# Weaving the top-32 searches of neighbouring score blocks, with the softmax in place in the score tile

## The chip, the core and the metric

The kernel runs on one core of one Trainium2 chip. The metric is the device time of one execution in microseconds. A core has five engines that each work through their own queue of instructions in order: TensorE (PE, matrix products; PEld is its weight load), VectorE (DVE), ScalarE (ACT), GpSimd (POOL) and SyncE (SP, which here only issues DMAs). A wait on a semaphore holds everything behind it on that engine.

## What is computed

Attention with a top-32 mask, then two feed-forward layers.

```
scores = scale * q @ k^T                       # 4 batches, 8 heads, 576 x 576, head size 64
kth    = 32nd largest score of each row
scores = where(scores >= kth, scores, -1e9); scores -= max
attn   = exp(scores) / (sum + 1e-9);  x = (attn @ v) as 2304 rows x 512
x = (sigmoid(x @ w_gate) * (x @ w_val)) @ w_out        # inner size 1536
x = relu(x @ w_in)^2 @ w_out2                          # inner size 2048
```

## The kernel before

The 2304 rows are 18 row tiles of 128. They are worked through in 12 chunks: chunks 0 to 5 hold one row tile each, chunks 6 to 11 two each. For each chunk, attention runs over four pairs of heads; one row tile with one head is a **unit**, 144 units in all, eight per row tile. While the two layers (the MoE, `moe32` for chunks 0 and 1, `moe` for the others) of one chunk run on PE, attention works on a later chunk. A scheduler sets the order of each engine's instructions from the program's priorities and dependencies; `attend` says how many units attention is ahead of the MoE.

A unit goes through these stations:

- `scores` (L357): PE multiplies queries and keys into PSUM, ACT copies the 128 x 576 scores into a tile `S` (L379). There are five such tiles (`SB`), and the keys (`kn`, L148) and values (`vm`, L191) that are prepared for later batches take theirs from the same five.
- `softmax` (L382): the **search** on DVE, seven steps: MAX8 (L392, eight largest of each row) four times and MATCH_REPLACE8 (L399, which strikes those eight out) three times between them. The first replacement reads `S` and writes a second tile `W` (three of them); the later steps read and write `W`. Each step waits for the one before it. A manual order (L394) keeps one unit's search whole: the first MAX8 of a unit comes after the last of the unit before.
- Still `softmax`: POOL makes a bias (L408), ACT writes Prelu of `S` into `W` (L411), which removes what lies below the 32nd, then Exp in `W` with the row sum (L413, or L427 in chunks 0 to 5).
- Chunks 0 to 5: `transpose` (L462) lets PE transpose `W` (L475, L477), and `values` multiplies with the values.
- Chunks 6 to 11 (`ci >= TCI`): `turn16` (L444) takes a reciprocal on DVE (L450), ACT writes the scaled probabilities as fp16 into the score tile `S` (L454), POOL scales `W` (L455) and writes the fp16 remainders into `S` too (L457), and a DMA on SP transposes them into `PT` (L459). `values16` (L500) then multiplies `PT` with the values on PE (L509), once per pair of heads and row tile, 48 times.

So before the change a late unit holds its `S` until the DMA transpose has read it, and its `W` until POOL's subtraction. In chunks 0 to 5 it holds `S` until the Prelu has read it and `W` until PE has transposed it. The generator `attention` (L1011) emits all this unit by unit. Its inner function `late` (L1126) places the late work by the search of the unit that is running: `turn` of the unit before behind the third MAX8, and `tail` (the value products) of the unit two before behind the last.

Of the kernel before, what the change touches and what calls it, by code (L numbers as in the profile page):

```python
# [8 lines left out]
F16 = mybir.dt.float16  # L9
BF16 = mybir.dt.bfloat16  # L10
F32 = mybir.dt.float32
# [3 lines left out]
AF = mybir.ActivationFunctionType  # L15
# [6 lines left out]
P = 128  # L22
TOPK = 32
# [40 lines left out]
LOA = 0  # L64
TCI = 6
SB = 5
PB = 10


# [4 lines left out]
def tile_topk_attention__then__two_moe_layers(  # L74
# [135 lines left out]
    def split_values(b, hp, n, vm, ve, om, oe, sm, after):  # L210
        sb = sm.bitcast(BF16)[:, 4:6]
        pn = ps_t.tile([P, 512], F32, tag="tr", name=f"vn_{n}")
        for x in range(2):
            mm = nc.tensor.matmul(
                pn[:, 0:1], ones, sb[:, x : x + 1], start=(x == 0), stop=(x == 1)
            )
            if x == 0:
                tc.add_manual_dep(mm.ins, after.name, NOSYNC, reason="summed by then")
        s, _ = pow2_scale(pn[:, 0:1], sm.bitcast(I32)[:, 4:5], s=vsc[:, b * NHP + hp])
        nc.gpsimd.memset(oe[ST:P, :, 1], 0.0)  # L220
        for o, t, r in ((om, vm, P), (oe, ve, ST)):
            nc.scalar.activation(o[:, :, 0], t, AF.Copy, scale=s)
            nc.gpsimd.tensor_scalar(t[0:r], t[0:r], s[0:r], 1.0, op0=ALU.mult, op1=ALU.mult)
            nc.gpsimd.tensor_tensor(o[0:r, :, 1], t[0:r], o[0:r, :, 0], op=ALU.subtract)
        d = dpool.tile([P, 2, 2, CB + 1, D], F16, name=f"vd_{n}", tag=f"vd_{n}")
        for j in range(2):
            nc.sync.dma_start(d[:, j, :, 0:CB], om[:, j])
            nc.sync.dma_start(d[:, j, :, CB], oe[:, j])
        vscr[(b, hp)] = d
# [19 lines left out]
                    segs.append([b, i * P + o, n])  # L249
        return segs  # L250

    last_max = []
    xfacs = {}

    xsmall = {}
# [1 line left out]
    def xfac(ci, b):  # L257


        if ci not in xfacs:  # L260
            bs_ = batches(ci)
            vf = vsc.bitcast(F32)
            xts_ = xsmall[ci] = mpool.tile([P, 8], I32, tag="xsc", bufs=3, name=f"ix_{ci}")
            ix = xts_.bitcast(F32)[:, 0:1]
            nc.vector.reduce_max(ix, vf[:, bs_[0] * NHP : (bs_[-1] + 1) * NHP, 1], axis=AX.X)

            nc.gpsimd.tensor_scalar(ix, ix, 2.0, None, op0=ALU.mult)
            fs = {}
# [12 lines left out]
            xfacs[ci] = ix, fs  # L281
        return xfacs[ci][1][b]

    class Pair:

# [93 lines left out]
            nc.scalar.copy(ss.rearrange("p (e s) -> p e s", e=2), sp[:, :, 0:HALF])  # L379
            return ss  # L380

        def softmax(self, j, i, ss, late=None):  # L382

            tt = self.tts[i]
            h = 2 * self.hp + j
            wk = apool.tile([P, S], F32, tag="W", bufs=3, name=f"W_{tt}_{h}")

            mx = apool.tile([P, 2, 8], F32, tag="mx", bufs=2, name=f"mx_{tt}_{h}")
            cur = ss
            marks = []  # L390
            for r in range(TOPK // 8):
                m8 = nc.vector.max(mx[:, min(r, 1)], cur)  # L392
                if r == 0 and last_max:
                    tc.add_manual_dep(  # L394
                        m8.ins, last_max[0].name, NOSYNC, reason="one row block at a time"
                    )
                marks.append(m8.ins)
                if r < TOPK // 8 - 1:
                    nc.vector.match_replace(wk, mx[:, min(r, 1)], cur, NEG)  # L399
                    cur = wk  # L400
            last_max[:] = [m8.ins]
            if late is not None:
                late(marks)
            bs = apool.tile([P, 8], F32, tag="bs", bufs=3, name=f"bs_{tt}_{h}")


            kth = mx[:, 1, 7:8]
            nc.gpsimd.tensor_scalar(  # L408
                bs[:, 1:2], kth, mx[:, 0, 0:1], SCALE, op0=ALU.subtract, op1=ALU.mult
            )  # L410
            nc.scalar.activation(wk, ss, AF.Prelu, bias=kth, scale=-1.0, alpha=1.0 / BIG)  # L411
            if self.ci >= TCI:
                nc.scalar.activation(  # L413
                    wk, wk, AF.Exp, bias=bs[:, 1:2], scale=-SCALE * BIG, accum_out=bs[:, 2:3]
                )

                for b, _, o, n in pieces(tt):
                    nc.gpsimd.tensor_scalar(
                        bs[o : o + n, 3:4],
                        bs[o : o + n, 2:3],  # L420
                        1e-9,
                        xfac(self.ci, b)[o : o + n, self.hp : self.hp + 1],
                        op0=ALU.add,
                        op1=ALU.mult,
                    )
                return ss, wk, bs
# [17 lines left out]
        def turn16(self, j, i, ss, wk, bs, summed):  # L444


            tt = self.tts[i]
            h = 2 * self.hp + j
            rz = bs[:, 4:5]
            rc = nc.vector.reciprocal(rz, bs[:, 3:4])  # L450
            if summed is not None:
                tc.add_manual_dep(rc.ins, summed.name, NOSYNC, reason="summed by then")
            pp = ss.bitcast(F16)
            nc.scalar.activation(pp[:, 0:S], wk, AF.Copy, scale=rz)  # L454
            nc.gpsimd.tensor_scalar(wk, wk, rz, 1.0, op0=ALU.mult, op1=ALU.mult)  # L455
            for o, f, e in ((S + ST, 0, SM), (S, SM, S)):
# [260 lines left out]
        nc.gpsimd.tensor_tensor(xs[:, 1], xt, xs[:, 0], op=ALU.subtract)  # L717
        return xs, ix


    class Moe:
        pass

    ahead = {}

# [285 lines left out]
    def attention():  # L1011
# [58 lines left out]
        def turn(n, summed=None):  # L1070
            pr, pi, j, i = units[n]
            pr.turn16(j, i, *work.pop(n), summed)

        def tail(n, after=None):
# [30 lines left out]
            if j == 1 and i == len(pr.tts) - 1:  # L1105
                if pr.ci < TCI:
                    pr.values()
                if pr.hp == NHP - 1:
# [4 lines left out]
                    else:  # L1113
                        xsp[pr.ci] = pr.xt, xfacs[pr.ci][0]

        head(0)
        for n, (pr, pi, j, i) in enumerate(units):
            late = None
            if pr.ci < TCI:
                with tc.high_priority(offset=int(up[0])):  # L1120
                    head(n + 1)
                    if n > 0 and units[n - 1][0].ci < TCI:
                        tail(n - 1)
            if pr.ci >= TCI - 2:

                def late(marks, n=n, pr=pr):  # L1126
                    if units[n - 1][0].ci >= TCI:
                        turn(n - 1, marks[2])
                    if pr.ci >= TCI:
                        head(n + 1)  # L1130
                        if units[n - 1][0].ci < TCI:
                            tail(n - 1)
                    while late_values:
                        split_values(*late_values.pop(0), marks[3])
                    if units[n - 2][0].ci >= TCI:
                        tail(n - 2, marks[3])

            work[n] = pr.softmax(j, i, ready.pop(n), late)
            yield
        turn(len(units) - 1)  # L1140
        for n in range(len(units) - 2, len(units)):
            tail(n)
        yield

    usc = []
# [144 lines left out]
```

## Time and profile before

| | us |
|---|---|
| three runs | 1264.15, 1261.6, 1263.55 |
| median | 1263.55 |
| span of the profiled execution | 1261.3 |
| profiled execution's own time | not given beside its span |
| PE busy | 1176.1 (93%) |
| DVE busy | 954.8 (76%) |
| ACT busy | 828.6 (66%) |
| POOL busy | 846.5 (67%) |

A busy share is a mean over stages with different limits, so it doesn't say what a change is worth in one of them. A matmul's end is modelled, and a part of PE's matmul records is missing, so that PE's counts of instructions are too low. A wait is put down to the instruction or DMA that ended it.

### The profile page before, as it was taken

What the parts mean: (1) busy time and instruction counts of PE and PEld (TensorE: products, weight loads), DVE (VectorE), ACT (ScalarE), POOL (GpSimd) and SP (SyncE); (2) the same over time, 40 slices, a digit from 0 to 9 for tenths busy, and PEclk for the clock granted to TensorE, in tenths of its full rate; (3) what the DMA queues carried; (4) which work ended last, traced back from release to release, by engine and by line L of the source; (5) the groups of instructions that cost most, each with busy time, mean ns of one, the idle gap of its engine ahead of it and who ended that gap; (6) DMA issues with size and microseconds to landing.
All of it is one profiled execution on the core that took longest, in us unless ns stands there. A gap on an engine that the chain in (4) does not pass through costs nothing.

```text
span 1261.3 us, 30690 instructions
## 1 busy us (share of the span) xinstructions
PE 1176.1 (93%) x11477; PEld 957.5 (76%) x11477; DVE 954.8 (76%) x1965; ACT 828.6 (66%) x1719; POOL 846.5 (67%) x1294
## 2 busy tenths in 40 slices
PE   6757989999889998899998999999999999999998
PEld 5536877987777877779787778877876887787775
DVE  6998789899977978899988899999789969110010
ACT  4998996577767676677776777776567657322122
POOL 1788774488876577797876987797678659425223
PEclk9986999999989999999999999999999999999999
DMA  7988762223344356665776575567434523200000
GB/s 188 366 298 275 260 199 81 59 76 90 113 131 130 81 125 159 143 136 130 137 157 133 125 181 115 127 140 158 77 73 97 116 54 60 53 2 1 17 1 18
DMA packets 243190, 153.94 MB, mean 122 GB/s; under 512 B 193120, under 2 KB 209504, under 8 KB 243040
## 3 DMA queue, kind: packets, MB, share of 16 engines
q1 hardware_dynamic: 243040, 151.97, 47.7%
q8 instruction: 91, 1.49, 0.5%
q14 instruction: 59, 0.48, 0.1%
HBM read 105.51 MB, written 18.09 MB: 98 GB/s over the span
## 4 chain that ended last, share of the span: by engine, by line
PE 67%; ACT 9%; POOL 7%; DVE 7%; DMA 5%; issue 3%; SPq 2%; POOLq 0%; ACTq 0%; DVEq 0%
PE ph L858 12%; PE acc L879 12%; PE acc L793 8%; PE pg L753 8%; PE pv L753 8%; PE sp L376 5%; PE xp L509 3%; DMA PT<-S 3%; DVE mx L392 2%; PE xp L536 2%; DVE W L399 2%; PE pg L912 1%; PE qpt L336 1%; PE ph L959 1%; PE acc L976 1%
## 5 line engine op out<-in xcount | busy, mean ns | idle before, releaser
L392 DVE MAX8 mx<-W 128x8 f32<-128x576 f32 x432 | 327.9, 759 | 11.2
L399 DVE MATCH_REPLACE8 W<-mx,W 128x576 f32<-128x576 f32 x288 | 213.8, 742 | 0.0
L858 PE MATMUL ph<-x,wi_w 128*128 128x256 f16 (+1 forms) x1920 | 190.9, 253 | 2.7 <-ACT x L832 2.6
L879 PE MATMUL acc<-w_w,rh 128*128 128x512 f16 x768 | 182.2, 379 | 0.9 <-POOL rh L871 0.9
L858 PEld LDWEIGHTS <-wi_w 128*128 128x128 f16 x1920 | 156.4, 99 | 29.0 <-issue 4.0
L753 PE MATMUL pg<-xs,wg_w 128*128 128x256 f16 (+1 forms) x1440 | 148.4, 254 | 1.1 <-ACT th L763 0.8
L753 PE MATMUL pv<-xs,wv_w 128*128 128x256 f16 (+1 forms) x1440 | 143.8, 252 | 5.1 <-DVE th L765 3.7
L376 PE MATMUL sp<-kst,qt 128*128 128x288 f32 x608 | 132.9, 330 | 6.5 <-ACT rh L869 2.5
L457 POOL TENSOR_TENSOR S<-W,S 128x512 f16<-128x512 f32 x192 | 137.0, 735 | 2.1
L379 ACT COPY S<-sp 128x576 f32<-128x576 f32 x144 | 91.8, 638 | 66.3 <-PE sp L376 39.7
L793 PEld LDWEIGHTS <-wo_w 128*128 128x128 f16 x1440 | 119.6, 99 | 19.2 <-issue 7.4
L411 ACT ACTIVATE W<-S,mx 128x576 f32<-128x576 f32 x144 | 111.8, 776 | 30.9 <-DVE mx L392 30.5
L753 PEld LDWEIGHTS <-wg_w 128*128 128x128 f16 x1440 | 118.9, 99 | 17.2 <-issue 1.4
L753 PEld LDWEIGHTS <-wv_w 128*128 128x128 f16 x1440 | 117.4, 98 | 18.1 <-issue 5.8
L765 DVE TENSOR_TENSOR th<-pv,th 128x512 f32<-128x512 f32 (+1 forms) x60 | 34.7, 579 | 125.4 <-PE pv L753 121.0
L879 PEld LDWEIGHTS <-rh 128*128 128x128 f16 x768 | 72.0, 98 | 73.3 <-POOL rh L871 1.2
L392 DVE MAX8 mx<-S 128x8 f32<-128x576 f32 x144 | 107.3, 745 | 25.9 <-ACT S L379 24.1
L793 PE MATMUL acc<-gh,wo_w 128*128 128x256 f16 (+1 forms) x1104 | 105.6, 250 | 4.7 <-ACT gh L768 2.6
L399 DVE MATCH_REPLACE8 W<-mx,S 128x576 f32<-128x576 f32 x144 | 106.9, 742 | 0.0
L455 POOL TENSOR_SCALAR W<-W,bs 128x576 f32<-128x576 f32 x96 | 71.6, 746 | 52.6 <-ACT S L454 47.8
L870 POOL TENSOR_TENSOR r<-r 128x512 f32<-128x512 f32 (+1 forms) x80 | 69.6, 869 | 54.8 <-ACT rh L869 54.1
L376 PEld LDWEIGHTS sp<-kst,qt 128*128 128x128 f32 x608 | 90.8, 192 | 17.5 <-issue 3.8
(246 smaller groups left out, 2331.5 us busy)
## 6 DMA issues: line engine op xcount, KB each, us to landing
kst<-ks SPq DMA_DIRECT2D x112, 288.0 KB, 3.1
v<-vd SPq DMA_DIRECT2D x32, 320.0 KB, 3.3
qn<-in_q_dram SPq DMA_DIRECT2D x128, 64.0 KB, 2.3
wi_r<-in_moe_w_in_dram SPq DMA_DIRECT2D x16, 512.0 KB, 6.2
w_r<-in_moe_w_out_dram SPq DMA_DIRECT2D x16, 512.0 KB, 4.5
v<-in_v_dram SPq DMA_DIRECT2D x56, 128.0 KB, 2.4
wg_r<-in_moe_w_gate_dram SPq DMA_DIRECT2D x12, 512.0 KB, 6.0
wv_r<-in_moe_w_val_dram SPq DMA_DIRECT2D x12, 512.0 KB, 7.3
```

Of the source, the lines that this page charges most:

```text
L376: nc.tensor.matmul(sp[:, e, 0:HALF], l, r, start=(x == 0), stop=(x == len(ops) - 1))
L379: nc.scalar.copy(ss.rearrange("p (e s) -> p e s", e=2), sp[:, :, 0:HALF])
L392: m8 = nc.vector.max(mx[:, min(r, 1)], cur)
L399: nc.vector.match_replace(wk, mx[:, min(r, 1)], cur, NEG)
L411: nc.scalar.activation(wk, ss, AF.Prelu, bias=kth, scale=-1.0, alpha=1.0 / BIG)
L455: nc.gpsimd.tensor_scalar(wk, wk, rz, 1.0, op0=ALU.mult, op1=ALU.mult)
L457: nc.gpsimd.tensor_tensor(pp[:, o : o + e - f], wk[:, f:e], pp[:, f:e], op=ALU.subtract)
L753: nc.tensor.matmul(pp[:, e * N : (e + 1) * N], wblk(wd, a, c, f0, P), xs[:, b_, c, :], start=(e == 0 and n == 0), stop=(n == 3 * KM - 1), ...
L793: nc.tensor.matmul(accs[d // 2][:, (d % 2) * N : (d % 2 + 1) * N], wblk("wo", a, f, d * P, P), gh[:, b_, e * N : (e + 1) * N], start=(f == ...
L858: nc.tensor.matmul(ph[:, e * N : (e + 1) * N], wblk("wi", a, c, f0, P), x2[:, b_, c, :], start=(e == 0 and n == 0), stop=(n == 3 * KM - 1) ...
L870: nc.gpsimd.tensor_tensor(r, r, r, op=ALU.mult)
L879: nc.tensor.matmul(acc2[i][:, 0:DM], gh[:, b_, e * N + i * P : e * N + (i + 1) * P], wblk("w2", a, f, 0, DM), start=(f == 0 and x == 0), s ...
```

## The change

The search is taken apart into single steps (`rank`), 0 to 6. `orders` lays the last three steps of one unit (4, 5, 6; `KA = 4`) alternately with the first of the next, so that DVE's order is: step 4 of the old unit, 0 of the new, 5 of the old, 1 of the new, 6 of the old, 2 of the new, 3 of the new. The manual order now asks only that step 0 of a unit come after step 4 of the one before. Prelu and Exp work in place in `S`. `W` serves the search alone. In chunks 6 to 11 the fp16 tile is a tile of its own, `pp`, out of the same three buffers as `W`. The reciprocal is tied to the fifth step after the unit's last one (`DTURN`), the value products to the fourteenth (`DTAIL`); both distances are those of before. In `mx`, three buffers take the place of two.

```diff
+WB = 3
+DTURN = 5
+DTAIL = 14
+KA = 4
...
-            wk = apool.tile([P, S], F32, tag="W", bufs=3, name=f"W_{tt}_{h}")
...
+        def rank(self, st, k):
+            r, e = divmod(k, 2)
+            m8 = st.mx[:, min(r, 1)]
+            if e == 0:
+                return nc.vector.max(m8, st.cur).ins
+            ins = nc.vector.match_replace(st.wk, m8, st.cur, NEG).ins
+            st.cur = st.wk
+            return ins
...
+            st.wk = apool.tile([P, S], F32, tag="W", bufs=WB, name=f"W_{tt}_{h}")
+            st.mx = apool.tile([P, 2, 8], F32, tag="mx", bufs=3, name=f"mx_{tt}_{h}")
...
+            wk, mx = st.ss, st.mx
...
-            nc.scalar.activation(wk, ss, AF.Prelu, bias=kth, scale=-1.0, alpha=1.0 / BIG)
+            nc.scalar.activation(wk, wk, AF.Prelu, bias=kth, scale=-1.0, alpha=1.0 / BIG)
...
-            pp = ss.bitcast(F16)
+            pp = apool.tile([P, 2 * S], F16, tag="W", bufs=WB, name=f"pp_{tt}_{h}")
...
+        def orders(n):
+            a = [(n - 1, k) for k in range(KA, 7)]
+            b = [(n, k) for k in range(KA)]
+            m = []
+            while a or b:
+                m += a[0:1] + b[0:1]
+                a, b = a[1:], b[1:]
+            return m
...
+            for u, k in orders(n):
+                if u in state:
+                    ins = units[u][0].rank(state[u], k)
+                    if k == 0 and prev3 is not None:
+                        tc.add_manual_dep(
+                            ins, prev3.name, NOSYNC, reason="two row blocks at a time"
+                        )
+                    if k == min(KA, 6):
+                        prev3 = ins
+                    if k == 6:
+                        ends[u] = len(seq)
+                    seq.append(ins)
```

How the order moves, first on DVE, in chunk 10 (row tiles 14 and 15; a name ends in row tile, head and a buffer number). Before, one unit's search after the other:

```order
L392 MAX mx_14_2_14314<-S_14_2_14236 128x8 [waits Activation_49]
L399 MATCH_REPLACE W_14_2_14313<-mx_14_2_14314,S_14_2_14236 128x576 [waits DVE_49]
L392 MAX mx_14_2_14314<-W_14_2_14313 128x8 [waits DVE_49]
L399 MATCH_REPLACE W_14_2_14313<-mx_14_2_14314,W_14_2_14313 128x576 [waits DVE_49]
L392 MAX mx_14_2_14314<-W_14_2_14313 128x8 [waits DVE_49]
L450 RECIPROCAL bs_15_1_14277<-bs_15_1_14277 128x1 [waits Pool_49]
L399 MATCH_REPLACE W_14_2_14313<-mx_14_2_14314,W_14_2_14313 128x576 [waits DVE_49]
L392 MAX mx_14_2_14314<-W_14_2_14313 128x8 [waits DVE_49]
L392 MAX mx_14_3_14344<-S_14_3_14331 128x8 [waits Activation_49]
```

Only the reciprocal of an earlier unit comes between the steps of one search. After the change, at the same unit:

```order
L393 MAX mx_14_2_14331<-S_14_2_14287 128x8 [waits Activation_49]
L394 MATCH_REPLACE W_15_1_14253<-mx_15_1_14254,W_15_1_14253 128x576 [waits DVE_49]
L458 RECIPROCAL bs_15_0_14294<-bs_15_0_14294 128x1 [waits Pool_49]
L394 MATCH_REPLACE W_14_2_14330<-mx_14_2_14331,S_14_2_14287 128x576 [waits DMAHW5_49,DVE_49]
L393 MAX mx_15_1_14254<-W_15_1_14253 128x8 [waits DVE_49]
L393 MAX mx_14_2_14331<-W_14_2_14330 128x8 [waits DVE_49]
L394 MATCH_REPLACE W_14_2_14330<-mx_14_2_14331,W_14_2_14330 128x576 [waits DVE_49]
L393 MAX mx_14_2_14331<-W_14_2_14330 128x8 [waits DVE_49]
L393 MAX mx_14_3_14396<-S_14_3_14349 128x8 [waits Activation_49]
```

Steps of two units alternate, and the first replacement of a unit now waits for a DMA (`DMAHW5_49`), the transpose that read its buffer before. Over the whole program 577 of 864 search steps stood directly behind the step that they read, and 291 do now; 79 replacements wait for a DMA, none did.

The second place is ACT's order in the same chunk, around the score copy. Before:

```order
L413 ACTIVATE W_14_0_13694,bs_14_0_13719<-W_14_0_13694,bs_14_0_13719 128x576 [waits Activation_49,Pool_49]
L379 COPY S_15_1_14153<-sp_15_1_14154 128x576 [waits DMAHW5_49,PE_49]
L763 ACTIVATE th_8_2_13281<-pg_8_2_13231,ix_8_10024 128x512 [waits PE_49]
L454 ACTIVATE S_14_0_13567<-W_14_0_13694,bs_14_0_13719 128x576 [waits DVE_49,Activation_49]
L411 ACTIVATE W_14_1_13810<-S_14_1_13712,mx_14_1_13811 128x576 [waits DVE_49]
```

The score copy waits for a DMA (`DMAHW5_49`) beside PE's products, and the fp16 copy (L454) writes a score tile.

After the change, at the same copy:

```order
L421 ACTIVATE S_14_0_13613,bs_14_0_13877<-S_14_0_13613,bs_14_0_13877 128x576 [waits Activation_49,Pool_49]
L531 ACTIVATE xs_9_12494<-xp_12_3_13733 128x128 [waits PE_49]
L531 ACTIVATE xf_12_3_13762<-xp_12_3_13733 128x128
L385 COPY S_15_1_13952<-sp_15_1_13953 128x576 [waits PE_49]
L419 ACTIVATE S_14_1_13726<-S_14_1_13726,mx_14_1_13854 128x576 [waits DVE_49]
L462 ACTIVATE pp_14_0_13945<-S_14_0_13613,bs_14_0_13877 128x576 [waits DMAHW4_49,DVE_49,Activation_49]
```

The score copy has lost its wait for a DMA (89 of 144 copies had one, 12 have one now); Prelu and Exp read and write `S`; the fp16 copy goes into `pp`.

## Rows read from the trace of the kernel before

**Rows 1.** The page, part 1: busy us (share of the span), instructions.

```profile
PE 1176.1 (93%) x11477; PEld 957.5 (76%) x11477; DVE 954.8 (76%) x1965; ACT 828.6 (66%) x1719; POOL 846.5 (67%) x1294
```

**Rows 2.** Busy us (instructions) per engine in four stretches, granted clock, DMA share, GB/s.

```profile
0.00:450.00 450.00, 388.96 (x3576) 330.11 (x3577) 386.11 (x758) 346.12 (x698) 300.72 (x411) 0.95 0.54 168
450.00:600.00 150.00, 137.12 (x1871) 117.11 (x1868) 130.74 (x299) 106.13 (x253) 117.11 (x214) 0.99 0.60 136
600.00:1100.00 500.00, 495.06 (x4826) 391.15 (x4825) 427.05 (x886) 338.68 (x710) 378.92 (x622) 1.00 0.54 113
1100.00:1261.00 161.00, 154.91 (x1212) 119.15 (x1210) 10.94 (x24) 37.63 (x60) 49.72 (x49) 0.99 0.02 8
```

**Rows 3.** Waits, 620 to 1100 us: us in total, times, longest.

```profile
DVE th L765 <- PE pv L753: 27.9, 8, 8.2
...
PE x2pq L825 <- ACT x L823: 1.5, 1, 1.5
```

**Rows 4.** PE's waits, 450 to 620 us.

```profile
PE kpt L164 <- DMA kn<-in_k_dram: 5.5, 3, 2.8
PE sp L376 <- ACT rh L869: 2.5, 1, 2.5
...
PE xp L509 <- DMA PT<-S: 1.2, 2, 0.7
```

**Rows 5.** ACT's longest wait, 450 to 620 us.

```profile
ACT S L379 <- DMA PT<-S: 16.6, 11, 2.4
```

**Rows 6.** DVE in order of time, two places: start us, us, instruction.

```profile
603.89 0.76 DVE L392 MAX8 mx<-W 128x8 f32<-128x576 f32 x1
604.56 0.74 DVE L392 MAX8 mx<-S 128x8 f32<-128x576 f32 x1
605.34 0.09 DVE L399 MATCH_VALUE_LOAD W<-mx,S 128x8 f32 x1
605.42 0.74 DVE L399 MATCH_REPLACE8 W<-mx,S 128x576 f32<-128x576 f32 x1
606.20 0.76 DVE L392 MAX8 mx<-W 128x8 f32<-128x576 f32 x1
...
610.18 0.74 DVE L392 MAX8 mx<-S 128x8 f32<-128x576 f32 x1
...
625.58 0.74 DVE L399 MATCH_REPLACE8 W<-mx,W 128x576 f32<-128x576 f32 x1
626.24 0.15 DVE L450 RECIPROCAL bs<-bs 128x1 f32<-128x1 f32 x1
```

**Rows 7.** The page, part 4: the chain that ended last, share of the span by line.

```profile
PE ph L858 12%; PE acc L879 12%; PE acc L793 8%; PE pg L753 8%; PE pv L753 8%; PE sp L376 5%; PE xp L509 3%; DMA PT<-S 3%; DVE mx L392 2%; PE xp L536 2%; DVE W L399 2%; PE pg L912 1%; PE qpt L336 1%; PE ph L959 1%; PE acc L976 1%
```

**Rows 8.** The 96 DMA transposes into PT, 450 to 1100 us.

```profile
DMA to landing us min/median/max: 3.2/3.4/5.4
```

**Rows 9.** ACT's fp16 copy and PE's value products of one unit.

```profile
608.85 0.76 ACT L454 ACTIVATE S<-W,bs 128x576 f16<-128x576 f32 x1
...
617.29 0.94 PE L509 MATMUL xp<-PT,v 128*64 128x128 f16 x27 [0.66 <-DMA PT<-S]
```

**Rows 10.** A unit of chunk 3 from its search's last step to PE's transposes.

```profile
291.12 0.76 DVE L392 MAX8 mx<-W 128x8 f32<-128x576 f32 x1
291.80 0.74 DVE L392 MAX8 mx<-S 128x8 f32<-128x576 f32 x1
291.91 0.78 ACT L411 ACTIVATE W<-S,mx 128x576 f32<-128x576 f32 x1 [1.01 <-DVE mx L392]
...
298.60 0.74 DVE L392 MAX8 mx<-S 128x8 f32<-128x576 f32 x1
...
300.76 0.60 PE L477 MATMUL tp<-ident,W 128*128 128x128 f32 x4
```

**Rows 11.** ACT's wait at the score copy, 0 to 340 us.

```profile
ACT S L379 <- PE sp L376: 10.8, 10, 2.7
```

More of the change, by code (lines that the diff above doesn't have):

```diff
@@ L250, in segments @@
         return segs
-    last_max = []
     xfacs = {}
@@ L282, in xfac @@
         return xfacs[ci][1][b]
+    class Moe:
+        pass
     class Pair:
@@ L380, in scores, with softmax_head, softmax @@
             return ss
-        def softmax(self, j, i, ss, late=None):
+        def rank(self, st, k):
[6 more added lines that the diff above has]
+            return ins
+        def softmax_head(self, j, i, ss):
             tt = self.tts[i]
             h = 2 * self.hp + j
-            wk = apool.tile([P, S], F32, tag="W", bufs=3, name=f"W_{tt}_{h}")
[L388 to L403, printed above, removed]
+            st = Moe()
+            st.ss = st.cur = ss
+            st.wk = apool.tile([P, S], F32, tag="W", bufs=WB, name=f"W_{tt}_{h}")
+            st.mx = apool.tile([P, 2, 8], F32, tag="mx", bufs=3, name=f"mx_{tt}_{h}")
+            return st
+        def softmax(self, j, i, st):
+            tt = self.tts[i]
+            h = 2 * self.hp + j
+            wk, mx = st.ss, st.mx
             bs = apool.tile([P, 8], F32, tag="bs", bufs=3, name=f"bs_{tt}_{h}")
@@ L425, in softmax @@
                     )
-                return ss, wk, bs
+                return wk, bs
             nc.scalar.activation(
@@ L442, in softmax, with turn16 @@
             return wk, ident
-        def turn16(self, j, i, ss, wk, bs, summed):
+        def turn16(self, j, i, wk, bs, summed):
             tt = self.tts[i]
@@ L718, in split_x @@
         return xs, ix
-    class Moe:
-        pass
     ahead = {}
@@ L1114, in tail @@
                         xsp[pr.ci] = pr.xt, xfacs[pr.ci][0]
-        head(0)
-        for n, (pr, pi, j, i) in enumerate(units):
-            late = None
-            if pr.ci < TCI:
+        def orders(n):
[6 more added lines that the diff above has]
+            return m
+        head(0)
+        state = {}
+        last = len(units)
@@ new lines, in attention, with turns, tails @@
+        seq, ends = [], {}
+        turned, tailed = set(), set()
+        def turns():
+            for u in sorted(work):
+                if u not in turned and units[u][0].ci >= TCI and ends[u] + DTURN < len(seq):
+                    turned.add(u)
+                    turn(u, seq[ends[u] + DTURN])
+        def tails(kinds):
+            for u in sorted(ends):
+                if u in tailed:
+                    continue
+                late = units[u][0].ci >= TCI
+                if late in kinds and u in (turned if late else work) and ends[u] + DTAIL * late < len(seq):
+                    tailed.add(u)
+                    tail(u, seq[ends[u] + DTAIL] if late else None)
@@ L1120, in attention @@
+        prev3 = None
+        for n in range(last + 1):
+            ci = units[min(n, last - 1)][0].ci
+            if ci < TCI:
                 with tc.high_priority(offset=int(up[0])):
                     head(n + 1)
[L1122 to L1136, printed above, removed]
@@ L1138, in attention @@
-            work[n] = pr.softmax(j, i, ready.pop(n), late)
-            yield
-        turn(len(units) - 1)
-        for n in range(len(units) - 2, len(units)):
-            tail(n)
+                    tails((False,))
+            if n < last:
+                pr, pi, j, i = units[n]
+                state[n] = pr.softmax_head(j, i, ready.pop(n))
+            for u, k in orders(n):
[10 more added lines that the diff above has]
+                    seq.append(ins)
@@ new lines, in attention @@
+            turns()
+            if ci >= TCI:
+                head(n + 1)
+                tails((False,))
+            while ci >= TCI - 2 and late_values:
+                split_values(*late_values.pop(0), seq[-1])
+            tails((True,))
+            if n > 0:
+                pr, pi, j, i = units[n - 1]
+                work[n - 1] = pr.softmax(j, i, state.pop(n - 1))
+            turns()
+            yield
+        for u in range(last):
+            if u not in turned and units[u][0].ci >= TCI:
+                turn(u)
@@ L1143, in attention @@
+        for u in range(last):
+            if u not in tailed:
+                tail(u)
         yield
```

## The prediction

> **What bounds the kernel now.** I read the busy times first [rows 1]: PE (TensorE) is busy for 93% of the span, DVE (VectorE) for 76%. A mean hides the stages, so the second view cuts the span in four [rows 2]. In 0 to 450 us PE leaves 450 - 389.0 = 61.0 us idle; in 450 to 600 it leaves 150 - 137.1 = 12.9; in 600 to 1100 only 500 - 495.1 = 4.9; in 1100 to 1261, where the last two chunks of the MoE run and no search is left, 6.1. The granted clock is 0.95 in the first stretch and 0.99 to 1.00 after. So after 600 us PE is full. DVE is busy for 427 of the 500 us there, but it also stands idle for 27.9 us until PE brings a `pv`, and the longest time that PE waits for anything is 1.5 us [rows 3]. A faster search can give nothing there; a slower one can cost.
>
> The time to win is PE's idle time before 600 us. In 450 to 620 us PE's longest waits are 5.5 us for keys (`kn`) to land, three times, and 2.5 us for ACT's `rh` before a score product; it waits 1.2 us, twice, for a transposed tile `PT` [rows 4]. ACT waits in the same stretch 16.6 us, 11 times, in front of the score copy (L379), until an earlier DMA transpose has read its score tile [rows 5]. `kn` takes its buffers from the same five score tiles, and everything behind the copy on ACT, `rh` too, waits with it.
>
> **The price of a step.** A search has seven steps: MAX8 four times, MATCH_REPLACE8 (with its MATCH_VALUE_LOAD) three times, each reading what the one before wrote. In [rows 6] such a pair stands 0.78 us apart from start to start (604.56 to 605.34, 605.42 to 606.20). A MAX8 that does not need the MAX8 in front of it starts after 0.67 (603.89 to 604.56), and a reciprocal behind a MATCH_REPLACE8 after 0.66 (625.58 to 626.24). So a step that follows its own predecessor costs 0.11 us more. No idle time shows this; it lies inside the busy spans.
>
> The Trainium skill, page "VectorE: DVE Perf Modes", section "The DRAIN you can't avoid", reports that eight copies took the same 13.88 us with a semaphore after each and with one at the end, so that chaining costs nothing extra. By that the weave would save nothing, and the sum below would lose its second term. The rows disagree with it here (0.78 against 0.67), and I go by the rows.
>
> **What the weave changes on DVE.** In the order of DVE's instructions I counted the steps that directly follow the step they depend on: 577 of 864 before, 291 after, since reciprocals and other work already stood between some, and since the weave hardly forms in chunk 4. That is 286 x 0.11 = 31.5 us less DVE time: 78 steps or 8.6 us in chunks 0 to 5, 66 or 7.3 us in chunks 6 and 7, 142 or 15.6 us in chunks 8 to 11. No instruction is added or removed.
>
> **What of it reaches the end.**
> - After 600 us: 0. The 15.6 us become more waiting of DVE for PE [rows 3].
> - Over the whole chain that ended last, the two search lines L392 and L399 hold 2% each [rows 7], some 50 us. They shrink as the search does: 31.5 of 144 units x 5.62 us (604.56 to 610.18 [rows 6]) = 809 us, 3.9%, so 2 us. Bounds: 0, and the 8.6 us of chunks 0 to 5 at full. I take **2 us**, as most of the early chain is ACT, POOL and DMA work on weights.
> - In 450 to 600 us the buffers matter more. The score tile, now also the softmax's tile, comes free after POOL's last subtraction (L457), not when the DMA transpose has landed, 3.2 to 5.4 us after its issue, median 3.4 [rows 8]. In ACT's order 89 score copies waited for a DMA before and 12 after. I take **8 us**: the 5.5 for `kn` and the 2.5 behind the blocked ACT [rows 4]. Bounds: 0 (the wait turns up elsewhere) and 12.9 (all idle time of the stretch).
> - What takes its place: the fp16 tile `pp` now takes one of the three `W` buffers, so a MATCH_REPLACE8 must wait for the DMA transpose of the unit four before; 79 of them have such a wait, none had one. Behind it on DVE stand two searches, not one. From the last step of unit n-4 to that step of unit n there are 20 steps. A unit's 5.62 us, less the mean saving of 31.5/144 = 0.22, are 5.40, or 0.77 a step, so 15.4 us. In the unit of [rows 6, 9] the last step ended at 603.89 + 0.76 = 604.65 and PE's products on `PT` could start at 617.29, 12.6 us later. `pp` has also to wait until the search that holds its buffer ends, seven steps or 5.4 us after the unit's own end, where the copy now started 4.2 us after it (608.85): 1.2 us more. That leaves 1.6 us spare, so I take 0 here; where POOL or the queue is late, it is a few tenths, in a stretch where DVE waits for PE anyway.
> - PE's value products (L509) are tied to the 14th step after the unit's last one, before as after. These 14 steps shrink from 11.2 to 10.8 us while `pp` comes 1.2 later: 1.6 us less margin at each of the 48 products. PE waited twice for that DMA up to now [rows 4], once for 0.66 us [rows 9]; I take 1.6 us for those two, **3 us** lost. Bounds: 0, and 48 x 1.6 = 77 us if every product stood right at its landing.
>
> The sum against the profiled execution, whose span is 1261.3 us: -2 - 8 + 3 = -7. The median of the runs shown, 1263.55, is 2.25 us above that span; I put this on both sides alike and forecast **1256.5 us**.
>
> **The rivals.**
> - *Late transposes (slower).* PE runs in order, so a `PT` that lands after its product's place in PE's queue stops the MoE too, after 600 us as well, where there is no idle time to hide it. For it: in [rows 9] PE already stood 0.66 us at such a product. Against it: from 620 to 1100 us PE's longest wait of any kind was 1.5 us [rows 3]. If a quarter of the 48 x 1.6 us is paid, 20 us in place of 3, the sum is +10, **1273.5 us**. It decides from the point where more than six of the 48 products wait the full 1.6 us (10 us, the whole gain).
> - *Score tiles held too long early (no change).* In chunks 0 to 5 the score tile was free after the Prelu; now PE's transposes read it. In [rows 10] a search's last step starts at 291.12, the Prelu ends at 292.69 and the transposes end at 301.36: 8.7 us longer, at one unit per 6.8 us (291.80 to 298.60) 1.3 of five tiles more. If that makes early the same 8 us of PE waits that the late relief takes away, the sum is +1, **1264.5 us**. Against it: up to 340 us ACT's score copy waits for PE, 10.8 us, and for no buffer of note [rows 11].
> - *All of it counts (more).* If DVE is the pace of the first 600 us, as its 386 of 450 us suggest [rows 2], the 8.6 and the 12.9 us come through whole: -8.6 - 12.9 + 3 = -18.5, **1245 us**.
> - *The weave saves nothing on DVE.* Then -8 + 3 = -5, **1258.5 us**; this is what the page above would give. The rows on the two spacings speak against it.
>
> **How the numbers follow.** A measurement of this kernel tells some 0.2%, 2.5 us, from no change. Chances: the forecast 0.42, late transposes 0.27, early score tiles 0.15, all of it 0.11, no saving on DVE 0.05. Of the forecast's own spread a seventh lies within 2.5 us of no change; the third rival and most of the fourth are faster; the early tiles are mostly no change. That makes faster 0.53, the same 0.18, slower 0.29. The range for 8 in 10 goes from just under the case where all counts, 1244, to a little over the slower rival, 1276. By itself the forecast's case would be 1250 to 1262.
>
> **What would show it.** Right: woven MAX8 pairs 0.67 us apart; ACT's 16.6 us in front of the score copy nearly gone; PE's idle time in 450 to 600 us down from 12.9 to about 5; PE's waits after 600 us still a few us; DVE waiting longer for `pv`. Late transposes would show as PE waiting at the value products for `PT<-pp` by tens of us. Early score tiles would show as ACT waiting in front of the copy for POOL or PE before 450 us. My forecast is wrong if PE's idle time before 600 us does not shrink, or if DVE stands at MATCH_REPLACE8 for DMA and PE behind it.

## The result, and the profile after

The change makes the kernel slower: 1275.1 us (median of 4 runs, 1273.21 to 1276.74) against 1262.57 for the kernel before on the same chip, a ratio of 1.0106 [1.0085, 1.0127]. (A ratio is estimated from all runs and can differ by up to 0.2% from that of the two medians; the brackets are its 95% interval.) That is some 13 us, outside what a measurement can take for no change, and on the other side of the forecast. The profiled execution took 1275.39 us, with a span of 1273.6.

The page of the changed kernel, part 1 (columns as in [rows 1]):

```profile
PE 1176.9 (92%) x11477; PEld 955.9 (75%) x11477; DVE 924.4 (73%) x1965; ACT 823.4 (65%) x1719; POOL 847.2 (67%) x1294
```

DVE's busy time has fallen by 30.4 us, as it was meant to, and the kernel is slower all the same. The four stretches (columns as in [rows 2]):

```profile
0.00:450.00 450.00, 383.58 (x3552) 324.95 (x3553) 383.50 (x772) 350.01 (x710) 300.87 (x414) 0.96 0.54 170
450.00:600.00 150.00, 136.98 (x1860) 116.44 (x1858) 128.69 (x299) 103.66 (x243) 117.94 (x216) 0.97 0.64 137
600.00:1100.00 500.00, 489.07 (x4733) 383.74 (x4731) 399.89 (x869) 329.33 (x704) 375.53 (x613) 1.00 0.50 110
1100.00:1273.00 173.00, 167.22 (x1340) 130.82 (x1338) 12.33 (x26) 40.37 (x65) 52.87 (x52) 1.00 0.03 10
```

PE's idle time in 450 to 600 us, 12.9 before, is 13.0: nothing was won there. From 600 to 1100 us it is 10.9, where it was 4.9, and from 0 to 450 us 66.4, where it was 61.0. ACT's waits in 450 to 620 us, answering to [rows 5]:

```profile
ACT S L419 <- DVE mx L393: 6.9, 7, 2.6
ACT pp L462 <- DMA PT<-pp: 6.4, 3, 3.0
ACT S L385 <- POOL pp L465: 5.2, 6, 1.8
```

The 16.6 us in front of the score copy for a DMA are gone, as forecast. In their place ACT waits for a search's end (L419, the Prelu), for a transpose to free the tile that the fp16 copy writes (L462), and for POOL to free a score tile. PE's longest waits from 620 to 1100 us, answering to [rows 3]:

```profile
PE sp L382 <- ACT S L385: 2.3, 3, 1.6
PE xp L517 <- DMA PT<-pp: 2.3, 3, 1.0
PE sp L382 <- DMA kst<-ks: 2.2, 3, 1.3
```

Many small waits, no large one: the loss has no single place on PE. One stop of ACT shows how such a wait comes about. This is ACT in order of time, then the PE instruction that waited (start us, us, instruction, idle time before it):

```profile
498.43 0.41 ACT L357 COPY qn<-qpt 128x256 f32<-128x256 f32 x1
501.86 0.77 ACT L462 ACTIVATE pp<-S,bs 128x576 f16<-128x576 f32 x1 [3.03 <-DMA PT<-pp]
502.54 0.62 ACT L385 COPY S<-sp 128x576 f32<-128x576 f32 x1
```

```profile
503.22 0.80 PE L382 MATMUL sp<-kst,qt 128*128 128x288 f32 x4 [1.51 <-ACT S L385]
```

The fp16 copy stands 3.03 us until a transpose has read the tile that it is to write, one of the three `W`. The score copy behind it in ACT's queue is late by as much, the next score product waits for that copy to empty its PSUM tile, and the MoE's products stand behind the score product.

### The profile page after: what moved, and what is told of

Its sections match the earlier page's. It is cut to its first block, busy times and chain, and to the rows that moved or that the text cites. A ratio compares the mean times of both kernels' runs of the same rounds, so it can differ in the third digit from the quotient of the medians.

```text
span 1273.6 us, 30668 instructions
## 1 busy us (share of the span) xinstructions
PE 1176.9 (92%) x11477; PEld 955.9 (75%) x11477; DVE 924.4 (73%) x1965; ACT 823.4 (65%) x1719; POOL 847.2 (67%) x1294
## 4 chain that ended last, share of the span: by engine, by line
PE 49%; DVE 10%; POOL 9%; DMA 8%; ACT 6%; issue 4%; SPq 2%; POOLq 0%; DVEq 0%; ACTq 0%
PE acc L884 8%; PE ph L863 8%; PE acc L798 7%; PE pg L758 6%; PE pv L758 6%; DMA PT<-pp 4%; DVE mx L393 4%; DVE W L394 4%; PE sp L382 3%; POOL pp L465 3%; PE ph L964 2%; PE acc L981 2%; PE xp L544 2%; PE xp L517 1%; PE pg L917 1%
## 5 line engine op out<-in xcount | busy, mean ns | idle before, releaser
L393 DVE MAX8 mx<-W 128x8 f32<-128x576 f32 x432 | 319.7, 753 | 5.4
L394 DVE MATCH_REPLACE8 W<-mx,W 128x576 f32<-128x576 f32 x288 | 213.8, 742 | 0.0
L863 PE MATMUL ph<-x,wi_w 128*128 128x256 f16 (+1 forms) x1920 | 196.9, 256 | 8.8 <-ACT x L837 7.8
L863 PEld LDWEIGHTS <-wi_w 128*128 128x128 f16 x1920 | 160.9, 101 | 34.4 <-issue 9.5
L758 PE MATMUL pg<-xs,wg_w 128*128 128x256 f16 (+1 forms) x1440 | 145.6, 253 | 0.0
L419 ACT ACTIVATE S<-S,mx 128x576 f32<-128x576 f32 x144 | 111.5, 774 | 48.9 <-DVE mx L393 46.8
L465 POOL TENSOR_TENSOR pp<-S,pp 128x512 f16<-128x512 f32 x192 | 136.9, 734 | 4.7
L394 DVE MATCH_REPLACE8 W<-mx,S 128x576 f32<-128x576 f32 x144 | 106.9, 743 | 0.3 <-issue 0.3
L463 POOL TENSOR_SCALAR S<-S,bs 128x576 f32<-128x576 f32 x96 | 71.9, 749 | 42.6 <-ACT pp L462 42.4
```

The source lines that it names most:

```text
L393: return nc.vector.max(m8, st.cur).ins
L394: ins = nc.vector.match_replace(st.wk, m8, st.cur, NEG).ins
L419: nc.scalar.activation(wk, wk, AF.Prelu, bias=kth, scale=-1.0, alpha=1.0 / BIG)
L758: nc.tensor.matmul(pp[:, e * N : (e + 1) * N], wblk(wd, a, c, f0, P), xs[:, b_, c, :], start=(e == 0 and n == 0), stop=(n == 3 * KM - 1), ...
L863: nc.tensor.matmul(ph[:, e * N : (e + 1) * N], wblk("wi", a, c, f0, P), x2[:, b_, c, :], start=(e == 0 and n == 0), stop=(n == 3 * KM - 1) ...
```

## The experiments

All times are compared as ratios to the kernel before, run on the same chip; 1% is 12.6 us. One ratio is uncertain by some 0.2%, a difference of two by some 0.3%, 3 to 4 us.

### Weave and buffers apart

Three kernels complete a square of four with the changed one. Without a weave:

```diff
-KA = 4
+KA = 7
```

> The changed kernel with KA = 7: the steps of a search no longer alternate with those of the next, the new buffers (softmax in place in the score tile, the fp16 tile out of W's three) stay. Of DVE's 864 search steps 566 stand right behind the step they read (before 577, changed kernel 291); 63 replacements still wait for a DMA transpose, 11 score copies do. Theory 'weave' (the 12.5 us come from the search being spread over ten steps of DVE, so that what waits for its end on ACT and PE waits longer): 1262 to 1266 us, ACT's idle time in front of the Prelu back from 48.9 towards 30.9 us. Theory 'buffers' (they come from the score tile that is held until POOL's subtraction and from the replacement that waits for the fp16 tile's transpose): 1273 to 1278 us, or above, as DVE loses its 30 us of shorter spacing too.

With the weave and the buffers of before:

```diff
-            nc.scalar.activation(wk, wk, AF.Prelu, bias=kth, scale=-1.0, alpha=1.0 / BIG)
+            nc.scalar.activation(wk, ss, AF.Prelu, bias=kth, scale=-1.0, alpha=1.0 / BIG)
...
-            pp = apool.tile([P, 2 * S], F16, tag="W", bufs=WB, name=f"pp_{tt}_{h}")
+            pp = ss.bitcast(F16)
```

> The changed kernel's woven search with the buffers of before: Prelu from the score tile into W, the fp16 tile in the score tile. 309 of 864 search steps stand right behind the step they read; no replacement waits for a DMA, 90 score copies do (before 89). Theory 'weave': 1273 to 1278 us, as slow as the changed kernel, with ACT's idle time in front of the Prelu still near 49 us. Theory 'buffers': 1260 to 1265 us, with the score copy's waits for the DMA transpose back (16.6 us in 450 to 620 us) and DVE's waits for pp gone.

And both edits together:

> The changed kernel's rewritten generator with neither: KA = 7 and the buffers of before. 567 of 864 search steps stand right behind the step they read, no replacement waits for a DMA, 90 score copies do. What is left against the kernel before is the order in which the parts of a unit are emitted and the third small tile mx. Theories 'weave' and 'buffers' both say 1262 to 1265 us, no change. If it is above 1268 us, a part of the loss comes from the new order of emission, and neither theory has the whole of it.

Measured: both edits 1264.0 us, 1.0026 [1.0012, 1.0040]; no weave 1257.45 us, 0.9972 [0.9953, 0.9990]; old buffers 1285.22 us, 1.0180 [1.0155, 1.0206]. So the new buffers by themselves **gain** 0.54% (6.8 us), and the weave **loses** 1.54% (19 us) with the old ones and 1.34% (17 us) with the new ones. "Buffers" as the cause is out. Rewriting the generator (with its third `mx` tile) costs 0.26%, 3 us, which no step of mine had. Two of the three times lie outside what either theory gave: the old buffers above both, no weave below both.

With the old buffers the weave waits for tiles too, in other places. ACT and DVE from 450 to 1100 us, without the weave first (DVE had no wait of note at L394 there):

```profile
ACT S L385 <- DMA PT<-S: 15.7, 13, 2.3
```

```profile
ACT S L385 <- DMA PT<-S: 53.7, 43, 3.3
...
DVE W L394 <- POOL S L465: 16.0, 13, 3.4
```

### Where the weave loses

`KA` becomes a pair, for chunks 0 to 5 and for 6 to 11: (4, 7), then (7, 4), then (4, 5).

```diff
+        def deep(n):
+            return KA[units[min(n, len(units) - 1)][0].ci >= TCI]
...
-            a = [(n - 1, k) for k in range(KA, 7)]
-            b = [(n, k) for k in range(KA)]
+            a = [(n - 1, k) for k in range(deep(n - 1), 7)]
+            b = [(n, k) for k in range(deep(n))]
```

> The changed kernel with the weave in chunks 0 to 5 only (KA = 4 there, 7 in chunks 6 to 11); the new buffers stay everywhere. In PE's order the value products of the last head pair of row tile 14 stand behind 854 us of matmul work, as without the weave; with the weave everywhere they stand behind 844, of row tile 12 733 in place of 743. Theory 'order' (the weave makes the scheduler place the late attention 7 to 12 us of work earlier on PE than DVE can really deliver it, and in-order PE waits): the loss lies in chunks 6 to 11, so 1249 to 1258 us, at or below the run without any weave (1257.5), since in that pair of traces the woven kernel was 7 to 9 us ahead at row tiles 3 and 4. Theory 'longer search anywhere' (a search takes 8.3 us from its first step to its last in place of 6.0, wherever it is woven): some of the loss stays, 1262 to 1268 us.

> The changed kernel with the weave in chunks 6 to 11 only (KA = 7 in chunks 0 to 5, 4 after); the new buffers stay everywhere. PE's order has the late value products as early as the changed kernel has them (844 us of work before those of row tile 14, 854 without the weave). Theory 'order': all of the loss and none of the early gain, 1272 to 1285 us. Theory 'longer search anywhere': part of the loss, 1264 to 1271 us.

> The changed kernel with two steps woven in place of three in chunks 6 to 11 (KA = 5 there): a search runs over nine steps of DVE's order in place of eleven (seven without a weave), so it should take about 7 us in place of 8.3. PE's order keeps the late value products as early as in the changed kernel (row tile 14 behind 844 us of work). Theory 'order': the loss stays nearly whole, 1271 to 1277 us, as the order is the same. Theory 'longer search' (the loss goes with how long a unit holds its score tile and W on DVE): about half of the 17 us is gone, 1263 to 1269 us.

Measured: early only 1260.46 us, 0.9992 [0.9979, 1.0004]; late only 1272.4 us, 1.0075 [1.0061, 1.0090]; early three and late two steps 1270.79 us, 1.0056 [1.0043, 1.0069]. Most of the loss lies in chunks 6 to 11, where `W` also serves the fp16 tile: the late weave alone costs 1.03% against the kernel without a weave (0.9972), 13 of the 17 us. Early, the weave neither wins nor loses that these runs can tell, and PE's idle time from 0 to 450 us is no longer with the weave (66.4 us) than without (71.7). The third run fell between the two theories and decided nothing.

### Is it the place in PE's order?

The weave moved the attention's products 7 to 12 us of work forward in PE's queue, and "order" was my first theory of how it loses. One kernel keeps the weave and puts them back (both flags below set; a tie to a step that isn't emitted yet is kept in a list and added when the step exists); one sets only the flag for the fp16 tile; one has no weave and moves the products forward; one sets both flags with `KA = 5`:

```diff
-                if u not in turned and units[u][0].ci >= TCI and ends[u] + DTURN < len(seq):
+                if u not in turned and units[u][0].ci >= TCI and (EARLY_TURN or ends[u] + DTURN < len(seq)):
...
+                    go = u in turned and (n >= u + 2 if EARLY_TAIL else ends[u] + DTAIL < len(seq))
```

> The changed kernel, woven everywhere as it is (KA = 4), but the generator emits a late unit's reciprocal and fp16 tile one search earlier and its value products one search earlier, where the kernel before has them in the program; the ties to the 5th and 14th step stay and are added once these steps exist. Nothing is added or removed. PE's order then has the last value products of row tile 14 behind 853 us of matmul work (changed kernel 844, without a weave 854), of row tile 12 behind 742 (733, 743). 392 of 864 search steps stand right behind the step they read (changed kernel 291). Theory 'order' (the loss is that attention's work stands 7 to 12 us of work too early in PE's queue): 1253 to 1262 us. Theory 'longer search' (the loss is that a woven search takes 8.3 us in place of 6.0): 1268 to 1277 us, as the changed kernel.

> As the run before it, but only the reciprocal and the fp16 tile are emitted one search earlier (so that the fp16 tile takes the W buffer of its own unit and not of the next one, whose search still runs); the value products are emitted late as in the changed kernel, and PE's order stays the early one (row tile 14 behind 844 us, row tile 12 behind 733). Theory 'order': 1269 to 1277 us, no better than the changed kernel. If the buffer that the fp16 tile has to wait for is the cause: 1255 to 1263 us.

```diff
-KA = 4
+KA = 7
...
-DTAIL = 14
+DTAIL = 16
```

> No weave at all (KA = 7, new buffers), with DTAIL = 16 in place of 14: the value products are tied to two steps later, and the generator therefore emits them one search later. A search takes 6.0 us as without a weave; PE's order becomes the early one (row tile 14 behind 843 us of matmul work, row tile 12 behind 733, as in the changed kernel). Theory 'order': slower than the same kernel with 14 (1257.5), by about the weave's 13 to 17 us, 1268 to 1276 us. Theory 'longer search': 1254 to 1260 us, no loss, as the search is not longer.

> As the first of these runs, with two steps woven in place of three (KA = 5). PE's order has row tile 14 behind 853 us, as without a weave; 462 of 864 search steps stand right behind the step they read. Theory 'order': 1252 to 1261 us, with a shorter search than three woven steps and less DVE time than none. Theory 'longer search': 1262 to 1269 us.

Measured: both put back 1269.14 us, 1.0067 [1.0054, 1.0080]; fp16 tile alone 1268.34 us, 1.0060 [1.0047, 1.0074]; no weave and the early order 1257.75 us, 0.9975 [0.9961, 0.9989]; two steps and both put back 1274.25 us, 1.0101 [1.0081, 1.0120]. **"Order" falls**: with the early order and no weave nothing is lost (0.9975 against 0.9972), and putting the order back helped no more than emitting the fp16 tile earlier, which leaves the order as it was. That emission did win 0.46%, less than the 1255 to 1263 us that I had asked of it if its tile were the whole cause. In those two kernels no wait of the fp16 copy on ACT ends with a `W` tile any more, though ACT stands in front of it longer in all (70.1 and 59.8 us from 450 to 1100 us, 39.2 in the changed kernel), and the replacements on DVE wait more for the transpose (17.4 us in the second, 8.4 in the changed kernel). That pointed to the tiles. The fourth run fits no theory: two woven steps came out slower than three.

### A fourth W tile

Room for it was made at the MoE's cost, so four kernels are compared among themselves:

```diff
-HIB = 4
+HIB = 3
...
-        ve = apool.tile([P, 2, D], F32, tag="we", bufs=3, name=f"ve_{n}")
+        ve = apool.tile([P, 2, D], F32, tag="we", bufs=2, name=f"ve_{n}")
...
-WB = 3
+WB = 4
```

> The changed kernel with room made in the on-chip memory: HIB = 3 in place of 4 (tiles of the MoE's activations) and two in place of three small tiles of the tag we. Woven (KA = 4), W still three tiles. 77 replacements wait for a DMA transpose (changed kernel 79). A control for the next run: no theory speaks of its own time; taking tiles from the MoE may cost some us, so 1274 to 1290 us.

> As the run before it, with a fourth W tile (WB = 4). 17 replacements wait for a DMA transpose in place of 77; PE's order stays within 2 us of work of it. Theory 'W tiles' (two searches at a time and the fp16 tile leave no W tile free, so that replacements on DVE and fp16 copies on ACT wait for one, with everything behind them): 10 to 16 us faster than three W tiles. Theory 'longer search' (the loss comes from each unit's work after the search being 2.3 us later): no change, within 3 us of three W tiles.

> The same room, no weave (KA = 7), three W tiles. Both theories: 12 to 18 us faster than the woven kernel with three W tiles, as without the room (1257.5 against 1275).

> The same room, no weave, four W tiles. Theory 'W tiles': little change against three (0 to 4 us faster, as one search at a time leaves a tile free), so that the woven kernel with four W tiles comes within 4 us of this one. Theory 'longer search': the weave's loss stays, 11 to 18 us between the woven kernel with four W tiles and this one.

Measured: woven, three tiles 1287.75 us, 1.0196 [1.0174, 1.0218]; woven, four 1270.84 us, 1.0076 [1.0061, 1.0092]; not woven, three 1270.14 us, 1.0065 [1.0045, 1.0084]; not woven, four 1267.12 us, 1.0051 [1.0033, 1.0068]. The fourth tile is worth 1.20%, 15 us, with the weave and 0.14% without. The weave costs 16.5 us with three tiles and 3 with four, which a difference of two runs can't tell from nothing. The waits from 450 to 1100 us, woven with three tiles:

```profile
ACT pp L462 <- DMA PT<-pp: 18.7, 8, 5.1
ACT pp L462 <- DVE mx L393: 9.4, 9, 1.4
...
ACT pp L462 <- DVE W L394: 5.8, 3, 3.6
...
DVE W L394 <- DMA PT<-pp: 4.8, 7, 1.1
```

and woven with four, where of all these one is left:

```profile
ACT pp L462 <- DMA PT<-pp: 1.2, 1, 1.2
```

These three lines on ACT are the fp16 copy that waits for a `W` tile: one that a transpose still reads, or one in which the next unit's search still runs. They add up to 33.9 us with three tiles and 1.2 with four. The changed kernel has 19.1 of it, the kernel without a weave 0.5:

```profile
ACT pp L462 <- DMA PT<-pp: 9.0, 5, 3.0
ACT pp L462 <- DVE mx L393: 8.6, 10, 2.2
...
ACT pp L462 <- DVE W L394: 1.5, 1, 1.5
...
DVE W L394 <- DMA PT<-pp: 8.4, 12, 1.4
```

```profile
ACT pp L462 <- DMA PT<-pp: 0.5, 1, 0.5
...
DVE W L394 <- DMA PT<-pp: 8.5, 10, 1.6
```

DVE's own wait for a tile is the same in both. But these lines count a wait by what ended it last. All of ACT's idle time in front of the fp16 copy (the number behind the second bar) is no longer with the weave than without; the changed kernel first, then the one without a weave, 450 to 1100 us:

```profile
L462 ACT ACTIVATE pp<-S,bs 128x576 f16<-128x576 f32 x96 | 74.3, 774 | 39.2 <-DMA PT<-pp 9.0 <-DVE mx L393 8.6 <-issue 7.5
```

```profile
L462 ACT ACTIVATE pp<-S,bs 128x576 f16<-128x576 f32 x96 | 74.5, 776 | 41.6 <-DVE bs L458 18.7 <-issue 17.9 <-ACT qn L357 1.9
```

Without the weave the copy stands there for its reciprocal (`bs`), and for what the profile doesn't name ("issue"). So the sums do not show that the weave's loss goes through ACT's queue. PE's idle time does follow the loss. From 450 to 1100 us (columns as in [rows 2]), without a weave, the changed kernel, and with room, woven, three tiles and four:

```profile
450.00:1100.00 650.00, 636.40 (x6733) 512.20 (x6733) 553.38 (x1167) 442.53 (x951) 493.65 (x829) 0.99 0.54 117
```

```profile
450.00:1100.00 650.00, 626.05 (x6589) 500.18 (x6588) 528.58 (x1167) 433.00 (x946) 493.48 (x828) 0.99 0.53 117
```

```profile
450.00:1100.00 650.00, 621.90 (x6549) 497.17 (x6548) 532.96 (x1176) 434.46 (x955) 493.51 (x829) 0.99 0.53 118
```

```profile
450.00:1100.00 650.00, 631.06 (x6642) 504.05 (x6642) 531.01 (x1177) 438.15 (x959) 495.81 (x832) 0.99 0.54 118
```

PE is idle for 13.6, 24.0, 28.1 and 18.9 us there.

### The same eight tiles, shared out otherwise, and a search that only ends later

```diff
-SB = 5
+SB = 6
-WB = 3
+WB = 2
...
-            pp = apool.tile([P, 2 * S], F16, tag="W", bufs=WB, name=f"pp_{tt}_{h}")
+            pp = apool.tile([P, 2 * S], F16, tag="S", bufs=SB, name=f"pp_{tt}_{h}")
```

> The changed kernel, woven, with its eight big tiles shared out otherwise: two W (the search alone) and six S, from which the fp16 tile now comes. No replacement waits for a DMA transpose any more (changed kernel 79); 13 score copies and 85 fp16 copies have such a wait. 302 search steps stand right behind the step they read. Theory 'W tiles': the search no longer competes with the fp16 tile, so most of the loss goes: 1255 to 1265 us. Theory 'longer search': 1270 to 1277 us, as the changed kernel.

> The same sharing without a weave (KA = 7). Theory 'W tiles': about as the three-W kernel without a weave, 1254 to 1262 us, and the woven one within 4 us of it. Theory 'longer search': the same time, and the woven one 11 to 18 us above it.

A kernel with no weave, whose Prelu is held back by three steps (`HOLD = 3`; `DTURN` and `DTAIL` are three more too):

```diff
+            if hold is not None:
+                tc.add_manual_dep(pl.ins, hold.name, SYNC, reason="held back")
...
+                k = ends[n - 1] + HOLD
+                late = pr.ci >= TCI and k < len(seq)
+                work[n - 1] = pr.softmax(j, i, state.pop(n - 1), seq[k] if late else None)
```

> No weave (KA = 7), the changed kernel's buffers with three W tiles, and in chunks 6 to 11 the Prelu of a unit really waits until the third step after the last of its search has run, as in a weave of three (about 2.1 us later); the ties of the reciprocal and of the value products are moved three steps back with it (DTURN = 8, DTAIL = 17). PE's order is the early one (row tile 14 behind 844 us of work). Each unit thus ends as late after its first step as a woven one, but only one search holds a W tile at a time. Theory 'longer search': 1268 to 1276 us. Theory 'W tiles': 1255 to 1263 us.

> As the held-back run (no weave, new buffers, three W tiles, DTURN = 8, DTAIL = 17), but the Prelu waits only for its own search again. Where the gain of that run (0.9904 of the kernel before, against 0.9972 without a weave) comes from the fp16 tile being written three steps later, when a W tile is free, this one is as fast: 1249 to 1254 us, and DVE's waits at a replacement for the transpose stay near 0. Where it comes from the held Prelu itself, 1255 to 1262 us.

Measured: shared out, woven 1270.37 us, 1.0065 [1.0048, 1.0081], and not woven 1271.36 us, 1.0076 [1.0058, 1.0093]; held back 1250.45 us, **0.9904 [0.9886, 0.9921]**; its ties alone 1257.53 us, 0.9959 [0.9945, 0.9972]. Where the search shares no tile with the fp16 tile, the weave costs nothing (-0.1%). Without the weave this sharing is itself slower by about 1% than five and three, which neither theory had said. ACT waits there 21.0 us, 7 times, for the values' DMA (`vm`, which takes a score tile), against 4.8 us in the kernel without a weave; whether that is the reason wasn't tried. As such a limit can also hide what the weave costs, the pairs with three and four `W` tiles are the stronger evidence. "Longer search", that a unit's later end costs the time, falls with the held-back kernel: every late unit goes on at least three steps after its search's end, and it is the fastest kernel of all.

The five pairs, woven less not woven, in one table, with PE's idle time from 450 to 1100 us in one profiled execution of each:

| tiles | woven | not woven | the weave costs | PE idle, woven / not, us |
|---|---|---|---|---|
| before's buffers | 1.0180 | 1.0026 | 1.54% | 31.4 / 20.4 |
| new buffers, three W | 1.0106 | 0.9972 | 1.34% | 24.0 / 13.6 |
| room, three W | 1.0196 | 1.0065 | 1.31% | 28.1 / 16.0 |
| room, four W | 1.0076 | 1.0051 | 0.25% | 18.9 / 14.5 |
| fp16 tile not in W | 1.0065 | 1.0076 | -0.11% | 22.5 / 21.0 |

Where the weave loses 17 to 19 us, it adds 10 to 12 us of idle time on PE in this stretch; the rest of the loss isn't placed.

## Why the prediction was wrong

- **The saving on DVE: right.** 31.5 us forecast, 30.4 measured, 0.106 us for each of the 286 pairs. The changed kernel's DVE in order of time shows both spacings, a woven pair 0.68 apart and a dependent one 0.78 apart (866.90 to 867.68), and once the wait of a replacement for its tile:

```profile
863.07 0.76 DVE L393 MAX8 mx<-W 128x8 f32<-128x576 f32 x1
863.75 0.74 DVE L393 MAX8 mx<-S 128x8 f32<-128x576 f32 x1
...
865.44 0.09 DVE L394 MATCH_VALUE_LOAD W<-mx,S 128x8 f32 x1 [0.23 <-DMA PT<-pp]
...
866.90 0.74 DVE L393 MAX8 mx<-W 128x8 f32<-128x576 f32 x1
867.68 0.09 DVE L394 MATCH_VALUE_LOAD W<-mx,W 128x8 f32 x1
```

  The rival that the weave saves nothing on DVE is out. The Trainium skill, page "VectorE: DVE Perf Modes", section "The DRAIN you can't avoid", reports of eight copies that a semaphore after each cost nothing extra. For these search steps the measurement differs, 0.78 against 0.68 us, and it decides.
- **What of it reaches the end: 2 us forecast, nothing seen.** The weave in chunks 0 to 5 alone gave 0.9992, without it 0.9972; and where the tiles are free the weave gains nothing either (0.25% and -0.11% in the table).
- **After 600 us, 0: wrong.** PE's idle time from 600 to 1100 us rose from 4.9 to 10.9 us. DVE's saved time did not become more waiting for PE's `pv` (27.9 us before, 24.3 after, from 620 to 1100 us). My own sign of being wrong came true as well: PE's idle time before 600 us did not shrink, it went from 73.9 to 79.4 us.
- **The buffers: right in size.** 8 us forecast, 6.8 measured without the weave and 9.3 with it (1.0180 to 1.0106). PE's idle time in 450 to 600 us falls there to 150 - 141.5 = 8.5 us, from 14.1 in the kernel that is only rewritten. In the changed kernel the weave took this back.
- **The value products: right.** 3 us forecast; PE waited 3.8 us for `PT` (1.5 in 450 to 620, 2.3 after), 1.2 before. The slower rival, late transposes, named nearly the right time (1273.5) by a mechanism that did not happen: it asked for tens of us at that place.
- **The step that failed: the `W` tiles, "1.6 us spare, so I take 0 here".** This is where the weave's 17 us come from: with a fourth tile 3 of 16.5 us are left. Three things went wrong in it. I followed a tile's way round to the *replacement*, on DVE, and found a stretch where DVE has time to wait. But the fp16 copy takes a tile out of the same three, and it is on ACT, in front of score copies and the MoE's activations. I saw that this copy "has also to wait until the search that holds its buffer ends", and priced it at 1.2 us of lateness for its own unit, not as a stop of ACT's queue. And I took the margin from one unit's times. A mean would not have warned me either: over the 96 late units a search of the changed kernel takes 8.2 us from its first step's start to its last step's end (6.2 without the weave, both worked out from the timeline), and an fp16 tile is held 8.5 us on average, which three tiles at 6.7 us a unit can carry. The waits are single ones: the fp16 copy's for a transpose and for a search's end come 5 and 10 times, up to 3.0 and 2.2 us long.
- **A term that was not there:** the rewritten order of emission, with the third `mx` tile, 0.26%.

With what was measured the sum is +3.3 (emission) - 6.8 (buffers) + 16.9 (weave) = +13.4 us, which is the measured ratio by construction. That the tiles make the last term is shown by the pairs with three tiles and with four; the pair with the fp16 tile elsewhere agrees. By which engine's queue it reaches PE is not shown. The trace shows one such case on ACT at 501.86 us, but ACT's idle time in front of that copy is as long without the weave; and where the fp16 tile is emitted earlier, the tile's wait is gone from ACT and longer on DVE, and 0.88% of loss stays against the kernel without a weave. Why two woven steps came out at once better (1.0056) and worse (1.0101) than three stays open.

## What to carry to other kernels

Where a change puts two units into a stage at a time, count every user of that stage's buffers, on every engine, and not only the one on the engine that is sped up: a wait for a tile also holds what is queued behind it. A margin of 1.6 us worked out of one unit's times was no margin here, and three tiles that suffice on average did not suffice. One more tile, tried with and without the change, tells whether buffers are the cause. And when one edit holds two ideas, measure the square of four: here one half gained 7 us and the other lost 17.

## What was not expected

Of the chip nothing: DVE's two spacings came out as the trace of before had them. Of the kernel, that holding work back made it faster: the held-back Prelu is worth 0.55% over the kernel that moves its ties alone, and the held-back kernel beats both the one before and the changed one, by 0.96% and 2.0%. Of ACT's idle time in front of the Exp (L421, L425 in the held-back kernel), 450 to 1100 us, most went: the kernel without a weave, the held-back one, and the one that moves its ties alone.

```profile
L421 ACT ACTIVATE S<-S,bs 128x576 f32<-128x576 f32 x94 | 72.8, 775 | 14.2 <-POOL bs L416 12.2
```

```profile
L425 ACT ACTIVATE S<-S,bs 128x576 f32<-128x576 f32 x95 | 73.6, 774 | 5.0 <-POOL r L879 0.4
```

```profile
L421 ACT ACTIVATE S<-S,bs 128x576 f32<-128x576 f32 x94 | 72.6, 772 | 1.4 <-POOL bs L416 1.0
```

When the Prelu goes later, POOL's bias is there by the time of the Exp, and ACT stands 9 us less in front of it. But it stands less still in the kernel that moves its ties alone, and that one gains only 0.13% over the kernel without a weave, within the noise. So this wait isn't what the held Prelu gains, and the reason stays open.
